# Rests of a local head on GpSimd, and the row maximum as a minimum

## The chip, the cores and the metric

The kernel runs on one core of a Trainium2 chip. The metric is the device time of one execution in microseconds; the kernel before takes 1069.08 us as the median of 3 runs (1068.36 to 1069.22). Engines are named as in the profile: PE is TensorE's matmul, PEld its weight load, DVE is VectorE, ACT is ScalarE, POOL is GpSimd, SP issues the DMAs.

## The reference

Attention over 8 batches of 8 heads, 512 local and 32 global tokens with head size 64, followed by a two-layer network on every token:

```
s_g  = scale * q_g @ [k_g, k_l]^T ;  out_g = softmax(s_g) @ [v_g, v_l]
s_l  = [scale * q_l @ k_g^T, where(|i - j| <= 32, scale * q_l @ k_l^T, -1e9)]
out_l = softmax(s_l) @ [v_g, v_l]          # softmax: exp(s - max) / (sum + 1e-9)
x = concat(out_g, out_l)                   # 8 * 544 tokens of 512
y = relu(x @ w_in)**2 @ w_out              # 512 -> 2048 -> 512, float32
```

## The kernel before

A local head is half a sequence of one head: 256 queries against 320 neighbouring keys and the 32 global ones, so there are 128 of them (t = 0 to 127), in 16 blocks of 8 (8 heads of one half of one batch). Each block gives 256 tokens for the network, which runs 9 steps behind (LAG): step t of the main loop (from line 587) works on attention of head t, finishes head t - 1, and does one eighth of the network for a block of tokens (m = t - 9). The global queries' scores are gathered beside this and handled in pieces (the g_ functions), spread over steps by a table of jobs that repeats every 16 heads.

Float32 accuracy comes from splitting. From head 16 on (heads before it are "plain"), a value is rounded to float32r (the rounded part, hi) and the remainder is kept as a second float32r number (the rest, lo); a product is the sum of three matmuls: hi by hi, hi by lo, lo by hi. split_head (line 125) does that for one head: ScalarE copies the whole loaded tile raw (128 x 864: 352 columns of k, 256 of q, 256 of v) into hi, and VectorE makes three rests:

- line 134: lo, 128 x 448, the rests of q (256 columns) and of the first 192 columns of v;
- line 135: the rest of k, written over the lower copy of k in hi (partitions 64 to 127, 352 columns), so that one matmul takes k's two parts at once;
- line 136: the rest of the global v, 32 x 64, likewise inside hi.

scores (line 139) then takes, for each half u of the queries, a matmul of hi's q with hi's k (`s<-hi`; it reads the k rest) and one of lo's q with hi's k (`s<-hi,lo`; it reads the q rest). av (line 226) reads the rests of v (`xa<-ph,lo` and the last `xa<-ph,hi`).

softmax1 (line 156) adds the mask to the scores and reduces the row maximum in one VectorE instruction for each half (`prob<-s,con`, with an accumulator read behind it), then multiplies both maxima by -scale with a TENSOR_SCALAR (`st<-st`). softmax2 (line 176) is ScalarE's exponential with that as bias. softmax3 (line 185) divides by the sum. pt_split and pt_rest (lines 202, 217) split the transposed probabilities: ph on ScalarE, pl and two more pieces of ph on VectorE.

The order on PE, ScalarE and VectorE is written out by hand: each engine's calls from step 17 on are kept in program order (class InOrder, FREE on line 28); before that the scheduler may choose. In one step PE does: transposes of head t - 1, scores of head t (`s`), the first half of gemm1 (`h`), the second half, av of head t - 1 (`xa`), global scores (`gs`), and gemm2 (`o`), with global pieces (`gxo`, `gt`) between. ScalarE does: pt_split of t - 1, the exponentials of t, the Relu of gemm1, x_evac of t - 1, hi of head t + 1, the copies of the global pieces, gh (the rounding for gemm2). VectorE: softmax1 of t, pt_rest of t - 1, softmax3 of t, the square or ScalarE does it, x_l, the rests of head t + 1, gl (line 478: r minus gh). POOL has four memsets and copies of plain global queries, and nothing after them.

Of the kernel before, what the change touches and what calls it, by code (L numbers as in the profile page):

```python
# [10 lines left out]
AF = mybir.ActivationFunctionType  # L11
ALU = mybir.AluOpType
# [8 lines left out]
QC, KC, VC = HALF, 352, 256  # L21
PK = QC + KC + VC
# [5 lines left out]
NPLAIN = 16  # L28

PLAN = [",,,b", "b,,,b", "b,,,b", "b,,b,", "b,,b,", "b,,b,", "b,,b,", "b,b,,b", "b,b,,b", "bb,bb,bb,bb", "bb,bb,bb,bb", "bbs,bb,bbs,bbs", "bbs,bbs,bbs,bbs", "bbs,bbs,bbs,bbs", "bbs,bbs,bs,s", "ss,s,s,s", "ss,s,s,s", "s,,s,", "s,,s,", "s,,s,", "s,,s,", "s,,s,", "s,,s,"]  # L30
FREE = (17, 17, 17)
LOOK = 2
SQ = (2, 3, 4, 5, 14, 15)
MUL = 9
# [3 lines left out]
def f(ap):  # L38
    return ap.bitcast(F32)
# [19 lines left out]
def attention_moe(  # L59
# [7 lines left out]
    out: bass.AP,  # L67
):
    nc = tc.nc
    pe, ve, ac = InOrder(tc, nc.tensor), InOrder(tc, nc.vector), InOrder(tc, nc.scalar)  # L70
    PSUM = bass.MemoryType.PSUM
    cp = ctx.enter_context(tc.tile_pool(name="cp", bufs=1))
    wp = ctx.enter_context(tc.tile_pool(name="wp", bufs=WCH))
# [8 lines left out]
    def plain(t):  # L82
        return t < NPLAIN
# [6 lines left out]
    def load_head(t):  # L90
        if plain(t):
            w_take(1)
            raw = wp.tile([P, 1024], F32, tag="w", name=f"raw{t}")[:, :PK]
        else:
            raw = p2.tile([P, PK], F32, tag="raw", name=f"raw{t}")
        if t == 0:
            nc.sync.dma_start(raw[:, : QC + KC], pk[t, :, : QC + KC])
        else:
            nc.sync.dma_start(raw, pk[t])
        heads[t] = dict(raw=raw)  # L100
# [24 lines left out]
    def split_head(t):  # L125

        hd = heads[t]
        raw = hd["raw"]
        if plain(t):
            return  # L130
        hi = p2.tile([P, PK], F32R, tag="hi", name=f"hi{t}")
        lo = p2.tile([P, QC + 192], F32R, tag="lo", name=f"lo{t}")
        ac.copy(hi, raw)
        ve.tensor_sub(lo, raw[:, KC : KC + QC + 192], f(hi[:, KC : KC + QC + 192]))
        ve.tensor_sub(hi[64:, :KC], raw[64:, :KC], f(hi[64:, :KC]))
        ve.tensor_sub(hi[32:64, PK - 64 :], raw[32:64, PK - 64 :], f(hi[32:64, PK - 64 :]))
        hd["hi"], hd["lo"] = hi, lo

    def scores(t):
# [12 lines left out]
    def scale(t):  # L152

        return 0.0625 if plain(t) else 0.125

    def softmax1(t):
        hd = heads[t]
        hf = (t // 8) % 2
        pr = prob[t % 2]
        st = p2.tile([P, 8], F32, tag="st", name=f"st{t}")  # L160
        for u in range(2):
            m = 2 * hf + u
            ve.tensor_tensor_reduce(
                out=pr[:, WIN * u : WIN * (u + 1)],
                in0=hd["s"][:, u, :],
                in1=masks[:, WIN * m : WIN * (m + 1)],
                scale=1.0,
                scalar=-3.0e38,
                op0=ALU.add,
                op1=ALU.max,  # L170
                accum_out=st[:, u : u + 1],
            )
        ve.tensor_scalar(out=st[:, 2:4], in0=st[:, 0:2], scalar1=-scale(t), scalar2=None, op0=ALU.mult)
        hd["st"] = st

    def softmax2(t):
        st = heads[t]["st"]
        pr = prob[t % 2]
        for u in range(2):
            w_ = pr[:, WIN * u : WIN * (u + 1)]  # L180
            ac.activation(
                out=w_, in_=w_, func=AF.Exp, scale=scale(t), bias=st[:, 2 + u : 3 + u], accum_out=st[:, 4 + u : 5 + u]
            )

    def softmax3(t):
        st = heads[t]["st"]
        pr = prob[t % 2]
        ve.tensor_scalar(out=st[:, 6:8], in0=st[:, 4:6], scalar1=1e-9, scalar2=None, op0=ALU.add)
        ve.reciprocal(out=st[:, 0:2], in_=st[:, 6:8])
        for u in range(2):  # L190
            w_ = pr[:, WIN * u : WIN * (u + 1)]
            if MUL <= t < NPLAIN:
                ac.activation(out=w_, in_=w_, func=AF.Copy, scale=st[:, u : u + 1])
            else:
                ve.tensor_scalar(out=w_, in0=w_, scalar1=st[:, u : u + 1], scalar2=None, op0=ALU.mult)

    def transposes(t):
        pr = prob[t % 2]
# [363 lines left out]
    def w_need(m):  # L562

        if m < 8:
            while w_next["bits"] < 8 * m + 8:
                n = w_next["bits"]
                w_pass()
                assert w_next["bits"] > n
        elif m < 16:
            while not set(range(4 * (m - 8), 4 * (m - 8) + 4)) <= whi.keys():  # L570
                n = w_next["split"]
                w_chunk()
                assert w_next["split"] > n, (m, w_next, w_bufs, sorted(w_used)[-1:])
# [14 lines left out]
    jobs = {}  # L588
    for t in range(NSTEP + LAG + 1):
        m = t - LAG  # L590
        ve.on, ac.on, pe.on = [t >= x for x in FREE]
        prev, run = 1 <= t <= NT, 0 <= m < NSTEP
        live, early = t < NT, t < NPLAIN
        if t < NPLAIN - 8:
            load_head(t + 8)
        if NPLAIN <= t + 2 < NT:
            load_head(t + 2)
        if run:
            w_need(m)
        if prev:  # L600
            transposes(t - 1)
        for job, *args in jobs.pop((t, 5), ()):
            job(*args)
        if live and not early:
            scores(t)
        if run:
            gemm1(m, 0)
        if prev:
            pt_split(t - 1)
        for job, *args in jobs.pop((t, 4), ()):  # L610
            job(*args)
        if live:
            softmax1(t)
            softmax2(t)
        if prev:
            pt_rest(t - 1)
        for job, *args in jobs.pop((t, 3), ()):
            job(*args)
        if 0 < m <= NSTEP and m % 8 == 1 and m > 8:
            evac(m // 8 - 1)  # L620
        w_tick(t, 0)
        if live and early:
            g_scores(t)
        if run:
            gemm1(m, 1)
        if prev:
            av(t - 1)
        if live and not early:
            g_scores(t)
        if early and t + 1 < NPLAIN:  # L630
            scores(t + 1)
        if live and not early:
            softmax3(t)
        if run:
            act1(m)
        if prev:
            x_evac(t - 1)
            if plain(t - 1):
                w_take(-1)
        if early:  # L640
            softmax3(t)
        w_tick(t, 1)
        if t + 1 < NT:
            split_head(t + 1)
        if live:
            if t % 2 == 1:
                g_evac(t)
            if t % 4 == 3 and t + 1 < NT:
                g_load(t + 1)
        elif t == NT:  # L650
            state["gs"] = None
        if live and t % 4 == 3 and (t // 8) % 2 == 1:
            d = t if t % 8 == 3 else t + 2
            for at, *job in (
                (d, 2, g_load_v, 0),
                (d + 1, 3, g_soft),
                (d + 1, 1, g_exp),
                (d + 2, 3, g_norm),
                (d + 2, 1, g_tr),
                (d + 3, 5, g_tr_last),  # L660
                (d + 3, 4, g_rest),
                (d + 3, 3, g_split_v, 0),
                (d + 3, 2, g_load_v, 1),
                (d + 3, 1, g_av, 0),
                (max(d + 4, 17), 3, g_x, 0),
                (d + 5, 2, g_split_v, 1),
                (max(d + 6, 17), 1, g_av, 1),
                (max(d + 7, 18), 3, g_x, 1),
            ):
                place, job, *args = job  # L670
                jobs.setdefault((at, place), []).append((job, t, *args))
        for job, *args in jobs.pop((t, 2), ()):
            job(*args)
        if m == NSTEP:
            for i in range(2):
                gemm2(m - 1, 0, (i,))
                gemm2(m - 1, 1, (i,))
                evac(NBLK - 1, (i,))
        elif m > 0:
            gemm2(m - 1, 0)  # L680
        for job, *args in jobs.pop((t, 0), ()):
            job(*args)
        if 0 < m < NSTEP:
            gemm2(m - 1, 1)
        if run:
            act2(m)
        w_tick(t, 2)
        for job, *args in jobs.pop((t, 1), ()):
            job(*args)
        if 0 < m <= 8:  # L690
            w_done(m - 1)
        w_tick(t, 3)
        if 8 * NGR - 2 <= m < 8 * NGR:
            cols = (slice(0, 224), slice(224, HALF))[m % 2]
            ac.copy(x_h[:, 0, :, cols], xg[:, :, cols])
            ve.tensor_sub(x_l[:, 0, :, cols], xg[:, :, cols], f(x_h[:, 0, :, cols]))
# [74 lines left out]
```

## Time and profile before

| | |
|---|---|
| median of 3 runs | 1069.08 us (1068.36 to 1069.22) |
| the profiled execution, first to last instruction | 1067.0 us |
| busy: PE, PEld | 1050.4, 941.7 us |
| busy: DVE, ACT, POOL | 856.3, 753.1, 3.9 us |
| granted TensorE clock | 1.000 |
| DMA moved | 96.78 MB |

The profile is of one execution. Its page has busy times, the span in 40 slices with the busy share of each in tenths, and the chain that ended last, followed back from the last instruction. A row of a group reads: line, engine, operation, written tile <- read tiles, shapes, count | busy us in total, mean ns of one | idle time of the engine just before them, and what ended it. A row of the timeline reads: start in us, length in us, engine, line, operation, tiles, shapes, count, and in brackets the idle time before it and what ended it; neighbours of one kind on an engine are merged, and the shape is that of one of them. Instructions of PE are pipelined: they overlap, and what counts is the distance between starts. All recorded operations of PE, ACT and DVE stand under line 52, the helper that issues them, so they are told apart by tiles.

### The profile page before, as it was taken

The page shows a single profiled execution, that of the slowest core. Times are in us where ns is not written, and L with a number is a line of the kernel's source. Part 1 is how long each engine was busy: PE and PEld are TensorE (multiplying, and loading weights), DVE is VectorE, ACT ScalarE, POOL GpSimd, SP SyncE. Part 2 cuts the span into 40 slices and gives each one's busy share as a digit, 9 for nine tenths or more (in the row PEclk, how much of TensorE's full clock was granted, in tenths as well). Part 3 has the DMA queues.
Part 4 walks back from the last instruction along what each step waited for, and adds up shares of the span by engine and source line. Part 5 has one row for each costly group of instructions (what it writes and reads, how often), then busy time and mean ns, then how long its engine had stood idle before and what let it go on. Part 6 is the DMA issues. An engine that isn't in the chain of part 4 may idle for free.

```text
span 1067.0 us, 21142 instructions
## 1 busy us (share of the span) xinstructions
PE 1050.4 (98%) x7568; PEld 941.7 (88%) x7568; DVE 856.3 (80%) x2687; ACT 753.1 (71%) x1901; POOL 3.9 (0%) x14
## 2 busy tenths in 40 slices
PE   7999999999999999999999999999999999999998
PEld 6776889999998989998999989999999989999896
DVE  5698988898888989988888888888888888874321
ACT  5898877778777776778777777777777787774322
POOL 1000000000000000000000000000000000000000
PEclk9999999999999999999999999999999999999999
DMA  9772132223222322222322222223221322201000
GB/s 372 310 263 74 57 106 76 71 80 98 68 89 64 103 65 83 74 91 77 94 71 82 86 72 76 90 66 100 78 89 55 94 86 66 88 29 33 13 20 20
DMA packets 54312, 96.78 MB, mean 91 GB/s; under 512 B 4288, under 2 KB 29376, under 8 KB 54208
## 3 DMA queue, kind: packets, MB, share of 16 engines
q1 hardware_dynamic: 54064, 95.37, 27.2%
q8 instruction: 60, 0.98, 0.4%
q14 instruction: 44, 0.36, 0.1%
q10 hardware_dynamic: 144, 0.07, 0.0%
HBM read 86.51 MB, written 8.91 MB: 89 GB/s over the span
## 4 chain that ended last, share of the span: by engine, by line
PE 87%; ACT 7%; DVE 4%; issue 1%; DMA 0%; ACTq 0%
PE o L52 33%; PE h L52 32%; PE xa L52 7%; PE s L52 6%; PE pt L52 5%; PE gxo L52 2%; PE gs L52 2%; ACT prob L52 1%; DVE prob L52 1%; ACT r L52 1%; ACT ph L52 1%; ACT hi L52 1%; ACT ot L52 1%; PE gt L52 1%; ACT sg L52 0%
## 5 line engine op out<-in xcount | busy, mean ns | idle before, releaser
L52 PE MATMUL h<-x_h,ws 128*128 128x256 f32 x2048 | 388.9, 283 | 0.0
L52 PEld LDWEIGHTS h<-x_h,ws 128*128 128x128 f32 x2048 | 327.0, 191 | 0.5
L52 PE MATMUL o<-ws,gh 128*128 128x512 f32 x1024 | 321.3, 395 | 0.0
L52 PE MATMUL h<-x_l,ws 128*128 128x256 f32 x1024 | 289.1, 282 | 0.1
L52 PEld LDWEIGHTS o<-ws,gh 128*128 128x128 f32 x1024 | 185.5, 188 | 34.6
L52 PE MATMUL o<-ws,gl 128*128 128x512 f32 x512 | 202.6, 396 | 0.0
L52 PEld LDWEIGHTS h<-x_l,ws 128*128 128x128 f32 x1024 | 195.9, 191 | 0.9 <-DVE x_l L52 0.4
L52 ACT CAST ph<-pt 128x256 fp32r<-128x256 f32 x448 | 141.1, 341 | 67.7 <-PE pt L52 60.8
L52 ACT ACTIVATE prob<-prob,st 128x224 f32<-128x224 f32 x270 | 127.8, 475 | 61.2 <-DVE st L52 59.1
L52 ACT ACTIVATE r<-h 128x512 f32<-128x512 f32 x136 | 81.4, 599 | 112.3 <-PE h L52 112.3
L52 PEld LDWEIGHTS o<-ws,gl 128*128 128x128 f32 x512 | 96.2, 188 | 22.7
L52 DVE CUSTOM_DVE_ANT_0 prob<-s,con 128x224 f32<-128x224 f32 x256 | 90.0, 386 | 24.5 <-PE s L52 23.2
L52 DVE TENSOR_TENSOR gl<-r,gh 128x512 fp32r<-128x512 f32 x128 | 87.9, 686 | 23.3 <-ACT gh L52 20.5
L52 ACT CAST hi<-raw 128x864 fp32r<-128x864 f32 x112 | 102.5, 915 | 1.4
L52 DVE TENSOR_TENSOR r<-h,r 128x512 f32<-128x512 f32 x82 | 56.7, 692 | 51.9 <-ACT r L52 50.6
L52 PE MATMUL xa<-ph,hi 128*64 128x128 f32 x448 | 87.3, 238 | 1.6 <-DVE ph L52 1.2
L52 DVE TENSOR_TENSOR hi<-raw,hi 64x352 fp32r<-64x352 f32 x224 | 82.5, 368 | 6.4
L52 ACT CAST gh<-r 128x512 fp32r<-128x512 f32 x128 | 79.1, 618 | 9.1 <-DVE r L52 8.7
L52 DVE TENSOR_TENSOR ph<-pt,ph 64x128 fp32r<-64x128 f32 x224 | 79.6, 355 | 7.0
L52 DVE TENSOR_TENSOR lo<-raw,hi 128x448 fp32r<-128x448 f32 x112 | 69.6, 622 | 15.3 <-ACT hi L52 12.5
L52 PE MATMUL pt<-con,prob 128*128 128x128 f32 (+1 forms) x512 | 78.2, 274 | 0.7 <-ACT prob L52 0.5
L52 DVE TENSOR_SCALAR prob<-prob,st 128x224 f32<-128x224 f32 x242 | 70.7, 334 | 4.1
(80 smaller groups left out, 1572.7 us busy)
## 6 DMA issues: line engine op xcount, KB each, us to landing
raw<-in_pk_dram SPq DMA_DIRECT2D x127, 432.0 KB, 3.2
wr<-in_w_dram SPq DMA_DIRECT2D x32, 512.0 KB, 7.9
gv<-in_vg_dram SPq DMA_DIRECT2D x32, 320.0 KB, 3.3
out_dram<-ot SPq DMA_DIRECT2D x32, 256.0 KB, 2.2
qr<-in_qg_dram SPq DMA_DIRECT2D x31, 64.0 KB, 2.8
out_dram<-ot SPq DMA_DIRECT2D x8, 64.0 KB, 1.7
con<-in_consts_dram SPq DMA_DIRECT2D x2, 224.0 KB, 5.1
raw<-in_pk_dram SPq DMA_DIRECT2D x1, 304.0 KB, 3.2
```

The lines of the kernel that those rows point to most:

```text
L52: r = method(*args, **kwargs)
```

## The change

POOL gets its own InOrder wrapper. The rests move from VectorE to POOL, the one of lo is cut into q and v, and the order becomes k, q, v, global v. The reduction in softmax1 multiplies by -scale and takes the minimum, so that its accumulator is already the bias and prob holds the negative scaled scores; the TENSOR_SCALAR goes, the exponential takes scale -1, and the reciprocal of the sum moves to other columns of st.

```
-FREE = (17, 17, 17)
+FREE = (17, 17, 17, 17)
...
-    pe, ve, ac = InOrder(tc, nc.tensor), InOrder(tc, nc.vector), InOrder(tc, nc.scalar)
+    pe, ve, ac, po = (InOrder(tc, e) for e in (nc.tensor, nc.vector, nc.scalar, nc.gpsimd))
...
         ac.copy(hi, raw)
-        ve.tensor_sub(lo, raw[:, KC : KC + QC + 192], f(hi[:, KC : KC + QC + 192]))
-        ve.tensor_sub(hi[64:, :KC], raw[64:, :KC], f(hi[64:, :KC]))
-        ve.tensor_sub(hi[32:64, PK - 64 :], raw[32:64, PK - 64 :], f(hi[32:64, PK - 64 :]))
+        po.tensor_sub(hi[64:, :KC], raw[64:, :KC], f(hi[64:, :KC]))
+        po.tensor_sub(lo[:, :QC], raw[:, KC : KC + QC], f(hi[:, KC : KC + QC]))
+        po.tensor_sub(lo[:, QC:], raw[:, KC + QC : PK - 64], f(hi[:, KC + QC : PK - 64]))
+        po.tensor_sub(hi[32:64, PK - 64 :], raw[32:64, PK - 64 :], f(hi[32:64, PK - 64 :]))
...
-                scale=1.0,
-                scalar=-3.0e38,
+                scale=-scale(t),
+                scalar=3.0e38,
                 op0=ALU.add,
-                op1=ALU.max,
+                op1=ALU.min,
                 accum_out=st[:, u : u + 1],
             )
-        ve.tensor_scalar(out=st[:, 2:4], in0=st[:, 0:2], scalar1=-scale(t), scalar2=None, op0=ALU.mult)
...
-                out=w_, in_=w_, func=AF.Exp, scale=scale(t), bias=st[:, 2 + u : 3 + u], accum_out=st[:, 4 + u : 5 + u]
+                out=w_, in_=w_, func=AF.Exp, scale=-1.0, bias=st[:, u : u + 1], accum_out=st[:, 4 + u : 5 + u]
...
-        ve.on, ac.on, pe.on = [t >= x for x in FREE]
+        ve.on, ac.on, pe.on, po.on = [t >= x for x in FREE]
```

More of the change, by code (lines that the diff above doesn't have):

```diff
@@ L188, in softmax3 @@
         ve.tensor_scalar(out=st[:, 6:8], in0=st[:, 4:6], scalar1=1e-9, scalar2=None, op0=ALU.add)
-        ve.reciprocal(out=st[:, 0:2], in_=st[:, 6:8])
+        ve.reciprocal(out=st[:, 2:4], in_=st[:, 6:8])
         for u in range(2):
@@ L192, in softmax3 @@
             if MUL <= t < NPLAIN:
-                ac.activation(out=w_, in_=w_, func=AF.Copy, scale=st[:, u : u + 1])
+                ac.activation(out=w_, in_=w_, func=AF.Copy, scale=st[:, 2 + u : 3 + u])
             else:
-                ve.tensor_scalar(out=w_, in0=w_, scalar1=st[:, u : u + 1], scalar2=None, op0=ALU.mult)
+                ve.tensor_scalar(out=w_, in0=w_, scalar1=st[:, 2 + u : 3 + u], scalar2=None, op0=ALU.mult)
     def transposes(t):
```

## The prediction

> **What bounds the kernel now.** I read the page first: busy time, slices, granted clock, the chain that ended last.
>
> ```profile
> span 1067.0 us, 21142 instructions
> PE 1050.4 (98%) x7568; PEld 941.7 (88%) x7568; DVE 856.3 (80%) x2687; ACT 753.1 (71%) x1901; POOL 3.9 (0%) x14
> PE   7999999999999999999999999999999999999998
> PEclk9999999999999999999999999999999999999999
> PE 87%; ACT 7%; DVE 4%; issue 1%; DMA 0%; ACTq 0%
> ```
>
> PE is busy in 1050.4 of 1067.0 us, in every slice but the first, at full clock, and the chain is 87% PE. Taking time from VectorE is worth nothing by itself: 16.6 us of PE idle is all that any change of the other engines could win, and part of that lies in the first slice. What the change does is decided at the places where PE waits for something that it touches. There are two: the score matmuls wait for the rests of a head (split_head), and the last attention-times-value matmul waits for a chain through softmax1. POOL (GpSimd) has nothing to do after the first heads: 14 instructions in all.
>
> The groups with shapes kept apart give the prices:
>
> ```profile
> L52 DVE TENSOR_TENSOR lo<-raw,hi 128x448 fp32r<-128x448 f32 x112 | 69.6, 622 | 15.3 <-ACT hi L52 12.5
> L52 DVE TENSOR_TENSOR hi<-raw,hi 64x352 fp32r<-64x352 f32 x112 | 58.5, 522 | 3.2
> L52 DVE TENSOR_TENSOR hi<-raw,hi 32x64 fp32r<-32x64 f32 x112 | 24.1, 215 | 3.2
> L52 DVE TENSOR_SCALAR st<-st 128x2 f32<-128x2 f32 x256 | 43.1, 169 | 11.3 <-ACT prob L52 4.2
> L52 DVE TENSOR_TENSOR gl<-r,gh 128x512 fp32r<-128x512 f32 x128 | 87.9, 686 | 23.3 <-ACT gh L52 20.5
> L275 POOL MEMSET qz<- 128x512 f32 x4 | 2.0, 525 | 10.0 <-PE gs L52 10.0
> L278 POOL COPY qz<-qr 128x128 f32<-128x128 f32 x4 | 1.2, 292 | 25.0 <-DMA qr<-in_qg_dram 25.0
> L122 POOL MEMSET sg<- 128x64 f32 x1 | 0.2, 152 | 0.0
> ```
>
> **Where PE meets the rests.** The timeline around the scores of head 69 (hi is ScalarE's rounded copy, then the rests, then PE):
>
> ```profile
> 506.38 0.92 ACT L52 CAST hi<-raw 128x864 fp32r<-128x864 f32 x1
> 507.20 0.62 ACT L52 CAST gh<-r 128x512 fp32r<-128x512 f32 x1
> 507.32 0.63 DVE L52 TENSOR_TENSOR lo<-raw,hi 128x448 fp32r<-128x448 f32 x1
> 507.98 0.77 DVE L52 TENSOR_TENSOR hi<-raw,hi 64x352 fp32r<-64x352 f32 x2
> 508.21 0.62 PE L52 MATMUL pt<-con,prob 128*128 128x128 f32 x4
> 508.65 0.34 PE L52 MATMUL s<-hi 128*128 128x224 f32 x1
> 508.83 0.27 PE L52 MATMUL s<-hi,lo 128*128 128x224 f32 x1
> 508.78 0.69 DVE L52 TENSOR_TENSOR gl<-r,gh 128x512 fp32r<-128x512 f32 x1
> ```
>
> hi is done at 507.30. The k rest, the first of the two in the 0.77 row, ends at 507.98 + 0.52 = 508.50, and PE's first score matmul starts 0.15 later, at 508.65, that is 1.35 behind hi; the second, which reads the q rest in lo, follows 0.18 later at 1.53. PE does not wait for the small third rest, which ends at 508.75: waits go by region, not by tile. Three other heads, 99, 70 and 71:
>
> ```profile
> 734.74 0.92 ACT L52 CAST hi<-raw 128x864 fp32r<-128x864 f32 x1
> 736.25 0.60 PE L52 MATMUL pt<-con,prob 128*128 128x128 f32 x4
> 737.01 0.34 PE L52 MATMUL s<-hi 128*128 128x224 f32 x1 [0.16 <-ACT sg L52]
> ...
> 513.72 0.91 ACT L52 CAST hi<-raw 128x864 fp32r<-128x864 f32 x1
> 515.58 0.60 PE L52 MATMUL pt<-con,prob 128*128 128x128 f32 x4
> 515.99 0.34 PE L52 MATMUL s<-hi 128*128 128x224 f32 x1
> ...
> 520.66 0.92 ACT L52 CAST hi<-raw 128x864 fp32r<-128x864 f32 x1
> 522.90 0.60 PE L52 MATMUL pt<-con,prob 128*128 128x128 f32 x4
> 523.26 0.35 PE L52 MATMUL s<-hi 128*128 128x224 f32 x1
> ```
>
> Head 71 is free: scores start 0.36 behind the transposes and 1.68 behind hi, the k rest long done. Heads 69 and 70 show 0.44 and 0.41, so 0.05 to 0.08 of wait; head 99 shows 0.76, a wait of 0.40, though the bracket names another releaser. In all three the first score stands 1.35 to 1.36 behind hi: the k rest is the wait that ends last. I followed this through all heads; it repeats with 16 heads. At places 0, 3, 5, 6 and 15 of the 16 (34 heads) the k rest decides, at place 13 sometimes, and everywhere else the first score stands 1.6 to 2.7 behind hi, for other reasons.
>
> **Part 1, the rests on POOL.** No row has a POOL instruction with two inputs, so I bound it. From the memsets: (525 - 152) / 448 = 0.83 ns a column and 99 ns fixed. The copy: (292 - 99) / 128 = 1.5 ns a column for one input and one output. Low end: 1.5, the second input free. High end: 3.0, each input at a copy's price. I take a copy plus one more stream at the memset's price, 2.34, since a second input adds one stream and not another output. Then k (352 columns) is 99 + 352 x 2.34 = 0.92 us, q (256) 0.70, v (192) 0.55, the last (64) 0.25. Three memsets together take
>
> ```profile
> 1.28 1.45 POOL L275 MEMSET qz<- 128x512 f32 x3
> ```
>
> 1.45 instead of 3 x 0.525, so one starts 0.06 before its forerunner ends. With VectorE's 0.02 to 0.03 from hi to the first rest and 0.15 from a rest to PE, the k rest frees PE at 0.03 + 0.92 + 0.15 = 1.10 behind hi (now 1.35) and the q rest at 0.03 + 0.92 - 0.06 + 0.70 + 0.15 = 1.74 (now in time, at 1.53). So the first matmul comes earlier and the second later: the wait moves from k to q. At places 0, 3 and 6 (20 heads) the second matmul is late by 1.74 - 1.54 = 0.20, which includes whatever was won on the first: 20 x 0.19 = +3.7 us, all on PE. At the free places it is due at 1.68 + 0.18 = 1.86 or later and 1.74 fits. Places 5 and 15 come below. With 1.5 ns, k takes 0.63 and q 0.48: ready at 0.81 and 1.23, and the waits go, most of all the 0.40 of place 3, where 0.31 is left to win: about -3 us. With 3.0 ns, k takes 1.16 and q 0.87: ready at 1.34 and 2.14, late by 0.60 at places 0, 3, 6 (+12 us), by about 0.27 at places 1, 7, 9, 11 and 13 (33 heads, +9 us) and by 0.1 at 5 and 15 (+1 us).
>
> The Trainium skill (GPSIMD Engine Reference, section Performance versus the Vector engine) gives a two-input add of 2048 fp32 columns 4497 ns on GpSimd; my estimate from that is 2.15 ns a column. By it q would be ready at about 1.62 and this term would be about +1.5 us instead of +3.7. No run here shows it yet.
>
> The v rest and the last one are done at about 0.03 + 0.92 + 0.70 + 0.55 + 0.25 - 0.19 = 2.3 behind hi. The first that reads them is attention times value a whole step later (head 68's at 503.7, against its hi at 498.2), so 3 us cover them. Nothing else stands in POOL's queue from head 16 on; only the next head's rests wait behind these. VectorE loses 0.63 + 0.77 = 1.4 us of a step of some 7.3, hidden by PE; gl can then start behind gh at 507.82 instead of 508.78, and its reader is a step away, so that is worth nothing.
>
> **Part 2, the softmax.** Removed: one TENSOR_SCALAR of 0.17 for each of 128 heads. Folding the scale into the reduction changes neither its shape nor its inputs, so I cost it at nothing. What it frees shows in the rows of head 68:
>
> ```profile
> 502.51 0.08 DVE L52 DVE_READ_ACCUMULATOR2_ANT st<- 128x1 f32 x1
> 502.94 0.17 DVE L52 TENSOR_SCALAR st<-st 128x2 f32<-128x2 f32 x1
> 503.02 0.42 DVE L52 TENSOR_TENSOR pl<-pt,ph 128x256 fp32r<-128x256 f32 x1
> 503.15 0.48 ACT L52 ACTIVATE prob<-prob,st 128x224 f32<-128x224 f32 x1 [1.29 <-DVE st L52]
> ...
> 504.07 0.22 PE L52 MATMUL xa<-ph,lo 128*64 128x128 f32 x1
> 504.36 0.30 PE L52 MATMUL xa<-ph,hi 128*64 128x256 f32 x1
> ```
>
> The first exponential can start behind the first accumulator read (502.59) instead of 503.15, 0.5 us earlier. In most steps ScalarE then waits longer for gemm1 and nothing comes of it. In the steps that make heads 5 and 15 of 16 ScalarE's row from the exponential to hi has no gap, so hi moves 0.5 us earlier, the wait of 0.07 ends, and even a q rest ready at 1.74 - 0.5 = 1.24 is in time: 14 x -0.07 = -1.0 us. In the same 14 steps PE holds 0.29 before its last value matmul, for the rest of ph on VectorE. Without the TENSOR_SCALAR that rest comes up to 0.2 earlier; I take 0.17, that is 14 x -0.17 = -2.4 us; bounds 0 and 14 x -0.27 = -3.8, the gap less the usual 0.02 to 0.06 spacing. Up to head 16 the order is not fixed by hand and may come out otherwise; PE is full there too, so nothing, within 1 us each way.
>
> **Sum.** +3.7 - 1.0 - 2.4 = +0.3 on a span of 1067.0, so 1067.3. The median of the runs shown is 1069.1, 2.1 more than this execution's span, for what lies around it: 1069.4 us. Less than 0.2% (2.1 us) either way is about what a measurement of this kernel can't tell from no change. With the terms' nearer bounds this case goes from 1064 to 1075.
>
> **Rivals.** *POOL is fast* (1.5 ns): 1067.0 - 3 - 1.0 - 2.4 + 2.1 = 1062.7. For it: the copy row. Against: a second input can't be free if it needs a stream of its own.
>
> *VectorE and POOL get in each other's way.* Place: gl, two SBUF inputs on VectorE. In odd places gh ends about 0.52 behind hi, inside POOL's k rest. If gl waits for that to end and then goes ahead of q, the q rest is ready at 1.74 + 0.69 = 2.43: late by 0.88 at place 3 (7 heads, 6 us), by 0.37 at 5 and 15 (14, 5 us), by some 0.55 at 9, 11, 13 and, through gvl, at 1 and 7 (35, 19 us), 0.2 at 0 and 6 (13, 3 us): +33 us, 1067.0 + 33 - 2.4 + 2.1 = 1100. If POOL keeps its turn instead, gl comes 1.5 us later and only crowded steps suffer, some +10. It decides as soon as gl or gvl falls between k and q at these places. The one meeting that the trace has:
>
> ```profile
> 24.78 0.29 POOL L278 COPY qz<-qr 128x128 f32<-128x128 f32 x1 [10.13 <-DMA qr<-in_qg_dram]
> 24.94 0.58 DVE L52 TENSOR_SCALAR prob<-prob,st 128x224 f32<-128x224 f32 x2
> 506.26 0.58 DVE L52 TENSOR_SCALAR prob<-prob,st 128x224 f32<-128x224 f32 x2
> ```
>
> Beside the copy the pair on VectorE takes the same 0.58 as alone, and the copy its usual 0.29. That speaks against, weakly: one input, 0.13 us of overlap. The Trainium skill speaks for it (SBUF — State Buffer, section Who interferes with whom): a VectorE instruction with two SBUF inputs and a GpSimd one that reads SBUF exclude each other for a whole instruction. The row neither bears that out nor refutes it.
>
> *POOL is dear* (3.0 ns): 1067.0 + 22 - 2.4 + 2.1 = 1089. Against: it would need each input to cost as much as a whole copy.
>
> **Chances.** My sum 0.40 (faster 0.10, same 0.21, slower 0.09, as the q term lies near 1.5 or above 4). Fast POOL 0.17, faster. Mutual waiting 0.30, slower. Dear POOL 0.08, slower. What early heads do if their order changes, 0.05 (0.02, 0.02, 0.01). Together: faster 0.29, same 0.23, slower 0.48. The single likeliest case is no change, though slower is the likeliest sign. The range takes in fast POOL at 1062 and mutual waiting at 1100.
>
> **What would show it.** Right: POOL groups near 0.92 and 0.70 us; at places 0, 3 and 6 the first score earlier behind hi than 1.35 and the second at about 1.74; the 0.29 hold of the value matmul down to about 0.1; gl at its 0.69, straight behind gh. Wrong: q rests starting long behind the end of k, or gl stretched or late beside POOL (mutual waiting); k above 1.1 or below 0.7; a PE wait at heads that were free.

## The result, and the profile after

The changed kernel takes 1100.23 us (median of 4 runs, 1099.12 to 1100.72); beside it the kernel before took 1069.03. The ratio is 1.0292, with a 95% interval of 1.0277 to 1.0306: 31 us slower. The profiled execution has a span of 1097.3 us, 30.3 more than before.

The page of the changed kernel, busy times and the chain that ended last by engine:

```profile
span 1097.3 us, 21206 instructions
PE 1063.6 (97%) x7568; PEld 946.3 (86%) x7568; DVE 734.2 (67%) x2223; ACT 753.6 (69%) x1901; POOL 340.6 (31%) x462
PE 59%; ACT 19%; POOL 13%; issue 6%; DVE 2%; DMA 1%; ACTq 0%; SPq 0%; DVEq 0%
```

VectorE lost 122 us of work, as meant, and POOL got 337. PE, 87% of the chain before, is 59% of it now, and POOL, which was not in it, has 13%. The waits for POOL, those of PE and of its weight loads:

```profile
PEld s L52 <- POOL lo L52: 34.6, 72, 0.9
PE s L52 <- POOL lo L52: 20.8, 65, 0.8
```

A matmul's wait stands at its weight load and again at the matmul, so the two rows overlap and are not added. They name one tile: lo, the q rest. The groups of POOL, and gl on VectorE:

```profile
L52 POOL TENSOR_TENSOR lo<-raw,hi 128x256 fp32r<-128x256 f32 x112 | 111.5, 995 | 8.8
L52 POOL TENSOR_TENSOR hi<-raw,hi 64x352 fp32r<-64x352 f32 x112 | 105.9, 946 | 589.3 <-ACT hi L52 589.3
L52 POOL TENSOR_TENSOR lo<-raw,hi 128x192 fp32r<-128x192 f32 x112 | 80.8, 722 | 0.0
L52 POOL TENSOR_TENSOR hi<-raw,hi 32x64 fp32r<-32x64 f32 x112 | 42.2, 377 | 8.8
L52 DVE TENSOR_TENSOR gl<-r,gh 128x512 fp32r<-128x512 f32 x128 | 115.7, 904 | 52.4 <-ACT gh L52 39.4
```

The k rest with 352 columns takes 0.95 us and the q rest with 256 takes 1.00: the shorter one is dearer. And gl, untouched by the change, went from 0.69 to 0.90. Both stretched where they meet. The timeline at head 70 (the last two POOL rests of lo are merged in one row):

```profile
526.22 0.91 ACT L52 CAST hi<-raw 128x864 fp32r<-128x864 f32 x1
527.21 0.94 POOL L52 TENSOR_TENSOR hi<-raw,hi 64x352 fp32r<-64x352 f32 x1 [5.07 <-ACT hi L52]
527.46 0.62 ACT L52 CAST gh<-r 128x512 fp32r<-128x512 f32 x1
528.11 0.69 DVE L52 TENSOR_TENSOR gl<-r,gh 128x512 fp32r<-128x512 f32 x1
528.23 1.71 POOL L52 TENSOR_TENSOR lo<-raw,hi 128x256 fp32r<-128x256 f32 x2
528.43 0.35 PE L52 MATMUL s<-hi 128*128 128x224 f32 x1
529.44 0.37 PE L52 MATMUL s<-hi,lo 128*128 128x224 f32 x1 [0.66 <-POOL lo L52]
529.65 0.27 PE L52 MATMUL s<-hi 128*128 128x224 f32 x1
```

Here gl starts 0.12 ahead of q and keeps its 0.69; q pays: PE gets it at 529.44, 2.3 behind hi and 1.0 behind the first score matmul, where 0.18 was usual. Before the change this head's second score stood 1.54 behind hi. At head 69 it is the k rest that is met:

```profile
519.11 0.94 POOL L52 TENSOR_TENSOR hi<-raw,hi 64x352 fp32r<-64x352 f32 x1 [5.42 <-ACT hi L52]
519.58 1.02 DVE L52 TENSOR_TENSOR gl<-r,gh 128x512 fp32r<-128x512 f32 x1 [0.55 <-ACT gh L52]
520.13 1.62 POOL L52 TENSOR_TENSOR lo<-raw,hi 128x256 fp32r<-128x256 f32 x2
521.24 0.37 PE L52 MATMUL s<-hi,lo 128*128 128x224 f32 x1 [0.24 <-POOL lo L52]
```

POOL was first, so gl is the one that stretches, to 1.02, and what is left of it when k ends is still ahead of q. The second score comes 2.2 behind hi. By place in the 16 heads it is now at 1.9 at place 0, 2.2 at 1, 3, 5, 7, 9, 11, 13 and 15, and 2.3 at 6 and 10. At 2, 8, 12 and 14 it stands where it stood. At 4 it comes 0.2 earlier (2.02 instead of 2.23), because a wait is gone. It stands in the list of before, and not in that of the changed kernel:

```profile
PEld gs L52 <- DVE sg L52: 1.9, 7, 0.4
```

In the seven steps with the scores of place 4, PE waited for a VectorE sum of global scores (sg) that stood behind the rests in VectorE's order. Between the hi of head 18 and that of head 127 the changed kernel loses 32.4 us, evenly; ahead of head 18 it is 2.9 us earlier than before.

### The profile page after: what moved, and what is told of

Read it like the earlier page. It is cut to its first block, busy times and chain, and to the rows that moved or that the text cites. A ratio compares the mean times of both kernels' runs of the same rounds, so it can differ in the third digit from the quotient of the medians.

```text
span 1097.3 us, 21206 instructions
## 1 busy us (share of the span) xinstructions
PE 1063.6 (97%) x7568; PEld 946.3 (86%) x7568; DVE 734.2 (67%) x2223; ACT 753.6 (69%) x1901; POOL 340.6 (31%) x462
## 4 chain that ended last, share of the span: by engine, by line
PE 59%; ACT 19%; POOL 13%; issue 6%; DVE 2%; DMA 1%; ACTq 0%; SPq 0%; DVEq 0%
PE h L52 30%; PE o L52 16%; POOL lo L52 7%; POOL hi L52 6%; ACT hi L52 6%; PE s L52 6%; ACT r L52 4%; PE xa L52 3%; ACT ph L52 2%; ACT prob L52 2%; ACT x_h L52 2%; PE pt L52 2%; PE gxo L52 1%; PE gs L52 1%; ACT ot L52 1%
## 5 line engine op out<-in xcount | busy, mean ns | idle before, releaser
L52 POOL TENSOR_TENSOR hi<-raw,hi 64x352 fp32r<-64x352 f32 x224 | 148.2, 662 | 598.1 <-ACT hi L52 589.3
L52 POOL TENSOR_TENSOR lo<-raw,hi 128x256 fp32r<-128x256 f32 x224 | 188.0, 858 | 8.8
L52 DVE TENSOR_TENSOR gl<-r,gh 128x512 fp32r<-128x512 f32 x128 | 115.7, 904 | 52.4 <-ACT gh L52 39.4
L52 PE MATMUL s<-hi,lo 128*128 128x224 f32 x224 | 62.9, 307 | 21.4 <-POOL lo L52 20.8
```

The costliest lines, as they stand in the source:

```text
L52: r = method(*args, **kwargs)
```

## The experiments

My theory after the result: a VectorE instruction with two SBUF inputs and a POOL instruction that reads SBUF exclude each other, the later one waiting, and this puts gl (and gvl) ahead of the q rest that PE waits for. The rival: POOL is late by itself, its k and q rests in a row take too long, and the stretched rows are a side show. Times are medians, ratios against the kernel before on the same chip.

**Each part alone.** e1 has the softmax part and the three old rests on VectorE; e2 the rests on POOL and the old maximum.

> Only the softmax part of the change: the rests stay on VectorE in the old order (q and v, k, global v). Both theories (mutual exclusion of gl and the rests on POOL; POOL late by itself) say that all of the loss goes: between 1063 and 1067 us. My term of the prediction for this part was -2.4, so 1066.7; the trace of the changed kernel shows head 18's hi 2.9 us earlier than before, and if that comes from this part the time is 1064 or less. If the fold of the scale made the reduction dearer it would be above 1069.

> Only the rests on POOL; the maximum and its TENSOR_SCALAR as before. Both theories: as slow as the change or slower by what the softmax part is worth, 1100 to 1106 us; second score matmul 2.2 to 2.3 us behind hi at most heads, as with the change.

e1: 1063.04 us, ratio 0.9949 (0.9937 to 0.9962), 5.6 us faster than before. e2: 1110.58 us, ratio 1.0393 (1.0377 to 1.0409), 42 us slower, more than I had expected. So the whole loss belongs to the rests, and the other part was a gain that they hid. The parts don't add up (+42 - 5.6 = +36, measured +31): with the softmax part hi comes about 0.3 us earlier, measured against PE, at places 5 and 15, as the position of the first score shows (1.62 behind hi in the changed kernel, 1.29 in e2), and there the late q rest costs less.

**gl with one SBUF input.** The changed kernel, edited in one line. h is gemm1's PSUM tile; m is at least 8 there, so gl is always made from h. What the kernel leaves out is the square in gl:

```
-        ve.tensor_sub(gl, r, f(gh))
+        ve.tensor_sub(gl, moe["hp"] if m >= 8 else r, f(gh))
```

> The changed kernel, but gl is made from the PSUM tile of gemm1 instead of r, so that this VectorE instruction has one SBUF input, with the same place, shape and about the same length (what is computed is wrong: the square is left out of the rest). Mutual exclusion: POOL's q rest falls back to about 0.74 us at every head but those beside gvl, gl to about 0.69, the q rest frees PE at about 1.9 behind hi instead of 2.2 to 2.3, and the time falls by about 20 us to 1080 (1076 to 1086). POOL late by itself: no change, 1097 to 1102.

1083.21 us, ratio 1.0135 (1.0121 to 1.0149): 17 us of the loss are gone, with gl at the same place and of the same shape, but for one input. The groups of e3:

```profile
L52 POOL TENSOR_TENSOR lo<-raw,hi 128x256 fp32r<-128x256 f32 x112 | 87.7, 783 | 8.8
L52 DVE TENSOR_TENSOR gl<-h,gh 128x512 fp32r<-128x512 f32 x128 | 88.5, 692 | 51.6 <-ACT gh L52 39.7 <-DMA out_dram<-ot 8.5
```

gl is back at 0.69 with POOL beside it, and q at 0.78; the second score comes 1.88 to 1.91 behind hi instead of 2.2 at places 3, 5, 6, 9, 11, 13 and 15, and stays at 2.21 at 1 and 7, where gvl still has two SBUF inputs. The rival said no change, so the meeting is worth these 17 us; it says nothing of the 20 that e3 still lies above e1, gvl's meetings among them.

**VectorE made to wait.** The changed kernel plus one instruction, ahead of gvl and gl in VectorE's order:

```
+        if NPLAIN <= t + 1 < NT:
+            gate = p2.tile([P, 1], F32, tag="gate", name=f"gate{t}")
+            ve.tensor_copy(out=gate, in_=f(heads[t + 1]["lo"][:, QC - 1 : QC]))
         for job, *args in jobs.pop((t, 2), ()):
```

> The changed kernel with one more VectorE instruction: a copy of one column of the q rest, put ahead of gvl and gl in VectorE's order, so that VectorE waits for POOL's q rest before it starts either of them. Nothing is left out; VectorE does more and waits longer. Mutual exclusion: the q rest is read alone at every head, 0.74 us, also beside gvl; the second score matmul at 1.88 to 1.93 behind hi at places 0, 1, 3, 6, 7, 9, 11 and 13; the time falls by 17 us as with gl from PSUM and by some 4 more for gvl: 1077 to 1083 us. POOL late by itself, or VectorE short of time: 1098 us or more.

1082.18 us, ratio 1.0126 (1.0109 to 1.0143): 18 us gained by adding work and a wait to VectorE. The groups of e9:

```profile
L52 POOL TENSOR_TENSOR lo<-raw,hi 128x256 fp32r<-128x256 f32 x112 | 82.5, 736 | 8.8
L52 DVE COPY gate<-lo 128x1 f32<-128x1 f32 x112 | 17.2, 154 | 148.9 <-POOL lo L52 148.9
L52 DVE TENSOR_TENSOR gl<-r,gh 128x512 fp32r<-128x512 f32 x128 | 117.2, 916 | 22.6 <-ACT gh L52 20.5 <-ACT ph L52 0.9 <-DMA out_dram<-ot 0.7
```

q is read alone: 0.74, at places 1 and 7 too, where the second score falls from 2.21 to 1.90. gl is as stretched as in the changed kernel (0.92, by the v rest now) and costs nothing: the stretch itself was never the loss, only which of the two comes second. The extra 4 us that I had expected for gvl did not come; the hold before the last value matmul grew, in the trace from 3.6 to 5.8 us in all (it now stands before the value matmuls of heads at places 0 and 6 too), as VectorE runs later.

**gl issued later.** The changed kernel with the subtraction of gl moved behind pt_rest of the next step, past POOL's burst:

```
         ac.copy(gh, r)
-        ve.tensor_sub(gl, r, f(gh))
+        moe["late"] = (gl, r, gh)
...
             pt_rest(t - 1)
+        gl_late()
```

> The changed kernel with gl issued later on VectorE: behind the rests of the transposed probabilities of the next step, so some 4 us behind hi and past all four rests on POOL; its reader is gemm2 half a microsecond or more after that. Nothing is left out. Mutual exclusion: as with gl from PSUM, POOL's q rest at about 0.74 to 0.78 us and the second score matmul at 1.88 behind hi except beside gvl; 1079 to 1086 us. If gl itself now comes late for gemm2, PE waits there and the time is higher. POOL late by itself: 1097 to 1102.

1092.68 us, ratio 1.0226 (1.0212 to 1.0240): 7.5 us of the loss are gone, about half of the least that I had expected. q is at 0.78 and gl at 0.69, as in e3, so the meeting with gl is gone; but a new wait stands in the list of e5:

```profile
ACT r L52 <- DVE gl L52: 23.3, 28, 1.8
```

r has one buffer, and ScalarE's next Relu needs it back from gl. At places 5 and 15 hi comes some 0.65 later against PE (the last transpose starts 0.92 behind it, in the changed kernel 1.58), which is more than it had won, and the second score waits again (1.87 behind a later hi). I had looked at gl's reader and not at its input.

**The same rests on VectorE.** The changed kernel with po replaced by ve in the four lines, so the same slices in the same order (k, q, v, global v):

> The changed kernel with its four rests in the same slices and order (k, q, v, global v), but on VectorE. Both theories: PE is freed by k at 0.03 + 0.52 + 0.15 = 0.70 behind hi and by q at about 1.15, so the waits of 0.05 to 0.4 us that the kernel before had on the k rest go: 3 to 5 us less than the softmax part alone, 1059 to 1064 us, faster than the kernel before. If the order did not matter it would equal the softmax part alone.

1060.18 us, ratio 0.9921 (0.9908 to 0.9935): 8.5 us faster than the kernel before, 2.9 faster than the softmax part alone, whose rests stand in the old order. The groups and head 51 of e4:

```profile
L52 DVE TENSOR_TENSOR lo<-raw,hi 128x256 fp32r<-128x256 f32 x112 | 47.7, 426 | 3.2
...
363.50 0.92 ACT L52 CAST hi<-raw 128x864 fp32r<-128x864 f32 x1
364.44 0.52 DVE L52 TENSOR_TENSOR hi<-raw,hi 64x352 fp32r<-64x352 f32 x1 [0.32 <-ACT hi L52]
365.04 0.60 PE L52 MATMUL pt<-con,prob 128*128 128x128 f32 x4
365.40 0.35 PE L52 MATMUL s<-hi 128*128 128x224 f32 x1
365.58 0.27 PE L52 MATMUL s<-hi,lo 128*128 128x224 f32 x1
```

Head 51 has place 3, where PE waited 0.40 before. Now the scores start 0.36 behind the transposes and 0.18 apart: no wait is left. The new slices with k first were worth having; the other engine was not. (e4 differs from e1 in the cut of lo as well as in the order; the two were not tried apart.)

**Rests shared out.** e6 has k and q on VectorE, v and the global v on POOL; e7 only k on VectorE and the other three on POOL.

> The rests of k and q on VectorE, in that order, those of v and the global v on POOL; softmax as changed. No read of these comes before the next step, so POOL's price is hidden. Mutual exclusion, earlier one first: VectorE's k rest starts 0.04 ahead of POOL's v rest and is read first, then v holds q back to about 1.1 and PE gets q at about 1.6 instead of 1.15; 1062 to 1067 us, slower than all four on VectorE (1060.2), and the q rest on VectorE stretched from 0.43 to 0.8 or more. Without mutual exclusion: equal to all four on VectorE or faster, 1058 to 1061.

> The k rest on VectorE, those of q, v and the global v on POOL at the same time; softmax as changed. Mutual exclusion: POOL's q can read only when VectorE's k is read (about 0.5 behind hi), so q is done at about 1.25 to 1.3, 0.3 later than its own price of 0.74 allows; in odd places gl may go ahead of it and make it 1.9. 1063 to 1080 us. Without mutual exclusion q is done at 0.07 + 0.74 = 0.81, before the k rest is needed: 1057 to 1060 us.

e6: 1060.20 us, 0.9923 (0.9909 to 0.9936). e7: 1059.62 us, 0.9916 (0.9903 to 0.9930). Both times are those that I gave to the case without exclusion, while the rows show exclusion. In e6 the q rest on VectorE went from 0.43 to

```profile
L52 DVE TENSOR_TENSOR lo<-raw,hi 128x256 fp32r<-128x256 f32 x112 | 73.8, 659 | 3.2
```

and in e7 the k rest on VectorE (64x352) and the q rest on POOL (128x256; the v rest, 128x192, follows it) meet at every head:

```profile
522.51 0.52 DVE L52 TENSOR_TENSOR hi<-raw,hi 64x352 fp32r<-64x352 f32 x1
522.61 1.03 POOL L52 TENSOR_TENSOR lo<-raw,hi 128x256 fp32r<-128x256 f32 x1 [4.63 <-ACT hi L52]
523.61 0.65 POOL L52 TENSOR_TENSOR lo<-raw,hi 128x192 fp32r<-128x192 f32 x1
...
530.89 0.75 POOL L52 TENSOR_TENSOR lo<-raw,hi 128x256 fp32r<-128x256 f32 x1 [5.91 <-ACT hi L52]
531.03 0.99 DVE L52 TENSOR_TENSOR hi<-raw,hi 64x352 fp32r<-64x352 f32 x1
531.60 0.88 POOL L52 TENSOR_TENSOR lo<-raw,hi 128x192 fp32r<-128x192 f32 x1
```

VectorE first (88 heads): its k takes the 0.52 that it takes alone, and the next instruction on POOL starts a full 1.00 after q's start. POOL first (24 heads): its next instruction starts 0.71 after q's start, and k takes 0.99. One rule with the order swapped: the first one loses nothing, so the two do not share, they take turns. The times did not follow because the loser is done early enough: from head 19 on, in e7 by 1.26 behind hi, in e6 by 1.3, or by 1.58 at places 9, 13 and 14, where PE comes for the second score at 1.86 or later. Elsewhere it comes at 1.48 or later, but for place 3 (7 heads, 1.20 in e7 and 1.35 in e6). I had priced the wait and not compared it with the slack.

**The softmax part from head 16 on.** As e1, with the maximum and the TENSOR_SCALAR kept for the plain heads:

> Only the softmax part, and only from head 16 on; the plain heads keep the maximum and the TENSOR_SCALAR, and all rests stay on VectorE in the old order. If the 5.6 us that the softmax part was worth are in the waits that I named (the value matmul and heads 5 and 15 of 16), about -2.5 to -3.5: 1065 to 1066. If all 5.6 lie there: 1063. The rest of the 5.6 is then the plain heads' (the trace of the softmax part alone has head 18's hi 1.0 us earlier).

1064.65 us, ratio 0.9962 (0.9949 to 0.9976): 4.0 us of the 5.6 lie behind head 16 and, by the medians, 1.6 in the plain heads. The intervals of e1 and e8 overlap, so the 1.6 is not clear of the noise; in the trace of e1 the hi of head 18 comes 1.0 us earlier than before.

## Why the prediction was wrong

**The failed step.** The sum let gl and the rests on POOL run side by side, each at its own length: gl at its 0.69, the q rest ready at 1.74. That overlap is the step that failed. What let it stand was the weighing of the one meeting that the trace of before had, a POOL copy and a VectorE pair that kept their lengths: I called it weak evidence against, gave mutual waiting 0.30 and made no change the single likeliest case. The rival's wait was what happened, with the signs that I had named for it (gl stretched, PE waiting at heads that were free): with its meeting taken away, at gl alone (e3) or for gvl and gl by a gate (e9), 17 to 18 us of the loss go; and e7 shows both orders. The one meeting had been no witness. None of the four copies in the trace of before meets a VectorE instruction with two SBUF inputs. One in the changed kernel does (the first two rows), and in e8 the copy meets the same pair, with the pair ahead (the last two):

```profile
34.94 0.69 DVE L52 SCALAR_TENSOR_TENSOR wf<-wr,wf 128x512 int32<-128x512 int32 x1
35.03 0.76 POOL L278 COPY qz<-qr 128x128 f32<-128x128 f32 x1 [9.97 <-DMA qr<-in_qg_dram]
...
24.38 0.61 DVE L52 TENSOR_SCALAR prob<-prob,st 128x224 f32<-128x224 f32 x2
24.46 0.40 POOL L285 COPY qz<-qr 128x128 f32<-128x128 f32 x1 [10.37 <-DMA qr<-in_qg_dram]
```

The copy takes 0.76 and 0.40 instead of its 0.29. The Trainium skill (SBUF — State Buffer, section Who interferes with whom) had the rule, that the two exclude each other while the second blocks, and the runs bear it out: gl 0.69 alone, 1.02 behind k; q 0.74 alone, and at head 70 not in PE's hands before 1.2 from its start. The later one does not wait for the very end: in e7 k as the later one is done 0.38 behind q's end, though it takes 0.52.

**The rival's price was 1100 and the time was 1100.2, partly by luck.** I let the whole of gl (0.69) stand between k and q, so q at 2.43. It came at 2.2 in odd places, because gl had started during k and, as I read the rows, had only its reading left when k was done. So places 1, 7, 9, 11 and 13 lost 0.34 to 0.40 and not 0.55, some 12 us instead of 19. Other places made up for it: place 6, with the rival's 0.2, lost 0.77, since gl came 0.12 ahead of q at 528.11, place 0 lost 0.39, and place 10, which the rival left free, 0.25.

**The sum was wrong without any meeting.** e9 against e1 is what the rests on POOL cost with q read alone: 1082.2 - 1063.0 = 19 us, where my terms had +3.7 (20 x 0.19 is 3.8). So of the 37 us between e1 and the changed kernel about half go with the meeting, and the other half is POOL being late by itself; that theory was wrong only in calling the stretched rows a side show. The price of an instruction was right: k 0.92 forecast, 0.95 measured; q 0.70 and 0.74; v 0.55 and 0.60, and (0.95 - 0.74) / 96 is 2.2 ns a column. By that the estimate of 2.15 from the Trainium skill (GPSIMD Engine Reference, section Performance versus the Vector engine) agrees with the trace. The spacing was wrong: POOL starts 0.08 behind hi, not 0.03; q starts 0.08 after k's end, not 0.06 before it (v does overlap q); PE follows 0.05 behind, not 0.15. Together the q rest frees PE at 1.88, not 1.74, which makes places 0, 3 and 6 late by 0.34 to 0.39 instead of 0.20: 7 us instead of 4. The rest was not in the sum at all: after a wait for the q rest the next score matmul follows 0.21 behind (529.44 to 529.65) and not 0.11, at some 70 heads 7 us; and the hold of the value matmul is 3.5 us more than in e1, of which 2.2 come with the gate (5.8 against 3.6). These two are read from traces and were not isolated by a run.

**The softmax part.** Right in sign, small in size: -1.0 and -2.4 forecast, -5.6 measured (e1). Behind head 16 it is -4.0 (e8) against -3.4. The plain heads' 1.6 I had put at nothing within 1 us. In e1 the hold of the value matmul falls from 3.9 to 2.3 us in all and the waits at places 5 and 15 are gone, as forecast. In the changed kernel that hold stayed at 3.6. In the step with the scores of place 4, PE comes to them 0.2 earlier there, and its last value matmul then starts 0.31 behind the one before it (0.11 in e1, 0.06 where nothing holds it): it meets the same chain sooner.

**What held.** VectorE's 1.4 us a step were worth little: taking them away ended the wait at place 4, a third place that the prediction had not seen, which is 7 x 0.21 = 1.5 us, and e4, e6 and e7, with more or fewer rests on VectorE, lie within 0.6 us. v and the global v were never late. The first score did come earlier, at 1.07 at place 3, and the wait did move from k to q. The sign with the highest chance was slower. The upper end of the range, 1100, was 0.2 us too low.

## What to carry to other kernels

Before moving work to an idle engine, list what the old engine runs at the moment when the moved work will run, and ask of each pair whether the two can read at the same time; an engine that is idle in the profile may not be free to read. Where an operand is waited for, reorder it on its own engine first: here that gave 3 us, and sharing k and the rest between two engines no more than that. A stretched instruction is no loss by itself; find who waits for the one that came second, and compare its new time with the slack there.

## What the runs showed of the hardware

- Two SBUF inputs on VectorE against a two-input subtraction on POOL: the later one waits until the earlier one has read, in both directions (e7: k on VectorE 0.52 when first and 0.99 when second; q on POOL, from its start to the next one's, 0.71 when first and 1.00 when second). With one input in PSUM the VectorE instruction keeps its 0.69 us (e3). One input alone is no general safeguard: in e8 a POOL copy took 0.40 instead of 0.29 behind a TENSOR_SCALAR with one tile in SBUF.
- On POOL, a subtraction of 256 columns takes 0.74 us alone, and one that follows over another number of partitions starts 0.08 us after the last one's end (the 8.8 us of idle before q are 112 times that), while v after q, both over 128, starts before q's end (in e7 at 523.61, where q ends at 523.64). Why was not tried.
- After a score matmul that waited for the q rest the next one starts 0.21 behind and not 0.11, with the rest on POOL (after, e9, e7) and on VectorE (e6, place 3). After one that waited for the k rest nothing is added: at place 3 before the change the second score follows 0.18 behind, as at places without a wait. Why was not tried.
